# A tile's sums of exponentials taken one turn ahead on VectorE, in a linear-attention and token-mixing block

## The chip, the cores and the metric

The kernel runs on one core of a Trainium2 chip. Its time is the device time of one execution in microseconds. The engines are TensorE (PE in the profile, with its weight loads as PEld), VectorE (DVE), ScalarE (ACT), GpSimd (POOL) and SyncE (SP), which issues most of the transfers. Each engine works through its own instructions in order and waits on semaphores for the others.

## What is computed

The input is x, 2048 tokens of 512 channels. The block adds a linear attention and then a token-mixing MLP, each to its own input, each behind a layer norm:

```python
q, k, v = split_heads(layernorm(x) @ wqkv)          # 32 heads of 16
pq, pk = q @ w_phi, k @ w_phi                       # per head
phi_q = concat(softmax(pq), softmax(-pq))           # 32 features; phi_k likewise
kv = phi_k^T v;  z = phi_k^T 1
o = (phi_q kv) / (phi_q z + 1e-6)
h = x + o @ wo
h2 = h + transpose(gelu(transpose(layernorm(h)) @ w1 + b1) @ w2 + b2)
```

What matters here is phi_q. For each token and head there are two softmaxes over 16 numbers, one of pq and one of -pq. Each needs an extreme (the largest, or the smallest, logit), the exponentials of the shifted logits, and their sum.

## The kernel before, in words

Tokens are cut into 16 tiles of 128. Every large product is made of three fp32r matmuls (high by high, high by low, low by high; `mm3`, lines 64 to 68), so most operands exist as a high part, written by ScalarE as a copy, and a low part, the difference, which is subtracted on VectorE or GpSimd.

A first stage makes k and v for all tiles, and q for the first ones. A second, the attention stage, is the loop at lines 711 to 755, in which this change lies. Behind it come the rest of the first MLP product and the whole second one, which take more than half of the time and are not touched.

The loop goes over `it` from 0 to 17; one pass is called a turn here. Inside it the order of TensorE, VectorE, ScalarE and GpSimd is the order in which the program is written (`manual_schedule`, line 447); only SyncE's transfers are placed by the scheduler. A turn works on several tiles at once:

- TensorE: the numerators `pn` of tile it-1 (`s_num`, line 591), the transposes `tr` of tile it's features (`s_tr`, 575), then one piece of work: half of a q projection (`q_half`, 692), or a tile's part of the first MLP product (`fill`, 678). Then `po`, the output projection of tile it-1 (`s_wo`, 609), and the rest of the work. `pn` and `po` share one PSUM buffer, so `po` waits until `ol` has read `pn`, and the next turn's `pn` waits until `h` has read `po`.
- ScalarE: the moments of tile it-2's h, `oh` (the high part of `pn`, 602), `pht` (the copy of the transposes, 582), the exponentials of one q tile (`q_exp`, 247), the normalized `hn` and its high part `hs` (636), and the high parts `whi` of streamed weights (`his`, 648).
- GpSimd: the division of tile it+1's features by their denominators (`s_pq`, 496: `eq<-eq,w`), `r` (634), the product `ez` of tile it+3's features with z (471), the low part of `hs` (line 62), and the shift of the negative logits (`negate`, 169).
- VectorE: for turns 0 to 4, 6 and 8 a q tile's two extremes and the shift (`logit_ops`, 151; lines 165, 166, 159). In each turn `ol`, the low part of the numerators (607). `wlo`, the low part of streamed weights (659). The two sums of a tile's exponentials (`q_sum`, 225: the instructions `smq<-eq` of line 230). The denominators of tile it+2 (`s_den`, 475: six instructions, the first `tr<-ez` at 486, the last `w` at 494), which read the sums of that tile. Then `h`, the residual sum of tile it-1 (623).

`flush(left)` and `flush(1)` issue the `wlo` of weights whose high part was ordered before: the first those left from the turn before, the second one more at the end of the turn.

The order of VectorE is what the change touches. `q["sum"]` counts the tiles whose sums were issued; six are taken in the first stage and one ahead of the loop, so the loop takes tiles 7 to 15. Their exponentials are made well before: tile 7's ahead of the loop, tile 8's in turn 1, tile 15's in turn 10. In turns 5 to 13 the sums of tile it+2 are taken just ahead of the denominators that use them:

```python
sm = q_sums(0) if q["sum"] <= it + 2 else []
ol = s_ol(it - 1) if 0 <= it - 1 < NT else []
run(ql[:2] + ol + ql[2:] if ql else sm[:1] + ol)
flush(left)
run(sm if ql else sm[1:])
```

So a turn with extremes runs: extreme, extreme, `ol`, shift, left `wlo`, sum, sum, denominators, `h`, `wlo`. A turn without: sum, `ol`, left `wlo`, sum, denominators, `h`, `wlo`.

Of the kernel before, what the change touches and what calls it, by code (L numbers as in the profile page):

```python
# [37 lines left out]
def block_kernel(ctx: ExitStack, tc: tile.TileContext, x, xT, wT, phic, wo, w1, b1, w2, b2,  # L38
# [130 lines left out]
    def negate():  # L169

        if MN:
            ev, mx, mn = MN.pop(0)
            nc.gpsimd.tensor_sub(mn, mn, mx)
            nc.gpsimd.tensor_sub(ev[:, :, 1], mn.unsqueeze(3).to_broadcast([P, NPR, 2, DH]), ev[:, :, 0])

    def turns(*lists):

        return [ops[i] for i in range(max(map(len, lists))) for ops in lists if i < len(ops)]

    def run(*lists):  # L180
        for op in turns(*lists):
            op()
# [42 lines left out]
    def q_sum(t):  # L225

        assert t < SUMS or t - SUMS in W, "a tile's sums would go where others are still wanted"
        SQ[t] = sums[:, t % SUMS]
        e = signs(EQ[t])
        return [lambda c=c: nc.vector.reduce_sum(SQ[t][:, :, 1 - c], e[:, :, c], axis=AX.X) for c in range(2)]  # L230

    q = {"mm": 0, "logits": 0, "exp": 0, "sum": 0}
# [6 lines left out]
    def q_logits(lag):  # L239
        n = q["logits"]  # L240
        if n < min(NT, q["mm"] - lag + NT * (q["mm"] == NT)):
            EQ[n] = big.tile([P, NG, P], F32, name="eq", tag="big")
            q["logits"] += 1
            return logit_ops(PS[n], EQ[n], n >= Q_EARLY)
        return []

    def q_exp(lag):
        n = q["exp"]
        if n < min(NT, q["logits"] - len(MN) - lag):
            exps(n, EQ[n])  # L250
            q["exp"] += 1

    def q_sums(lag):
        n = q["sum"]
        if n < min(NT, q["exp"] - lag + NT * (q["exp"] == NT)):
            q["sum"] += 1
            return q_sum(n)
        return []
# [212 lines left out]
    def s_ez(t):  # L471
        EZ[t] = az.tile([P, NG, P], F32, name="ez")
        nc.gpsimd.tensor_mul(EZ[t], EQ[t], zB)  # L473
# [22 lines left out]
    def s_pq(t):  # L496
        nc.gpsimd.tensor_mul(heads(EQ[t]), heads(EQ[t]), W[t].rearrange("p g c h -> p (g c h)").unsqueeze(2).to_broadcast([P, 2 * H, DH]))  # L497
# [77 lines left out]
    def s_tr(t):  # L575
        PHT[t] = ak.tile([P, NG, P], F32, name="pht")
        ptr = ps_t.tile([P, 8, P], F32, name="tr").rearrange("p (r c) (a s) -> p r (c a) s", r=2, a=2)
        for g in range(NG):
            for r, rows in enumerate(HALF):
                nc.tensor.transpose(ptr[:, r, g, :], EQ[t][rows, g, :], ident[rows, rows])  # L580
        for r in range(2):
            nc.scalar.activation(PHT[t][:, :, r * 64:r * 64 + 64], ptr[:, r], AF.Copy)

    def s_kv():

        pt = banks("pt")[:, 0, 0:2]
        for b in range(2):
            nc.tensor.transpose(pt[:, b, :], kvS[:, 2 * b:2 * b + 2, :].rearrange("p n f -> p (n f)"), ident)
        nc.scalar.activation(kvB, pt, AF.Copy)

    def s_num(t):

        pn = banks("pn")[:, :, 0:2]
        for b in range(2):
            for c in range(4):
                for r, rows in enumerate(HALF):
                    cols = slice(32 * c, 32 * c + 32)
                    nc.tensor.matmul(pn[cols, r, b, :], kvB[rows, b, cols], PHT[t][rows, 4 * b + c, :],
                                     start=True, stop=True, skip_group_check=True)
        oh = ak.tile([P, 2, 2, P], F32R, name="oh")  # L600
        ol = ak.tile([P, 2, 2, P], F32R, name="ol")
        nc.scalar.activation(oh, pn, AF.Copy)
        OS[t] = oh, ol, pn

    def s_ol(t):
        oh, ol, pn = OS[t]
        return [lambda: nc.vector.tensor_sub(ol, pn, oh)]

    def s_wo(t):
        oh, ol, _ = OS.pop(t)  # L610
        PO[t] = po = banks("po")[:, 0].rearrange("p a s -> p (a s)")
        for j in range(4):
            mm3(po, oh[:, j // 2, j % 2, :], ol[:, j // 2, j % 2, :], woh[:, j, :], wol[:, j, :], j == 0, j == 3)

    def s_x(t):
        HT[t] = ak.tile([P, D], F32, name="h", bufs=4)
        nc.sync.dma_start(HT[t], x[t * P:(t + 1) * P, :])
# [8 lines left out]
    def s_moments(t):  # L626

        junk = ak.tile([P, D], F32, name="hj", bufs=1)
        nc.scalar.activation(VE[t][:, 1:2], VE[t][:, 2:3], AF.Copy, scale=-1.0 / D)
        nc.scalar.activation(junk, HT[t], AF.Square, bias=VE[t][:, 1:2], accum_out=VE[t][:, 3:4])  # L630
        nc.scalar.activation(VE[t][:, 0:1], VE[t][:, 3:4], AF.Identity, scale=(1.0 + EPS) / D, bias=eps2)

    def s_rstd(t):
        nc.gpsimd.tensor_tensor(r2[:, t:t + 1], VE[t][:, 0:1], mhalf[:, :1], op=ALU.pow)

    def s_hn(t):
        hn = ak.tile([P, D], F32, name="hn")
        nc.scalar.activation(VE[t][:, 1:2], VE[t][:, 1:2], AF.Copy, scale=r2[:, t:t + 1])
        nc.scalar.activation(hn, HT[t], AF.Identity, scale=r2[:, t:t + 1], bias=VE[t][:, 1:2])
        HN[t] = big.tile([P, 2, D], F32R, name="hs", tag="big")  # L640
        split(HN[t][:, 0], HN[t][:, 1], hn, nc.gpsimd)
# [6 lines left out]
    def his():  # L648
        while COMING:
            LATER.append(COMING.pop(0))  # L650
            _, raw, wh_ = LATER[-1]
            nc.scalar.activation(wh_, raw, AF.Copy)  # L652

    def flush(n=None):
        if n is None:
            his()
        for _ in range(len(LATER) if n is None else min(n, len(LATER))):
            wl_, raw, wh_ = LATER.pop(0)
            LO.append(nc.vector.tensor_sub(wl_, raw, wh_).ins)  # L659
# [18 lines left out]
    def fill(p, pool=None):  # L678

        t = FN[p]  # L680
        FN[p] = t + 1
        if FL[p] <= t:
            fill_load(p)
            flush()
        if t == 0:
            PU[p] = [pool.tile([P, D], F32, name="pu", tag="pu") for _ in range(2)]
        a, b = WI[p, t - t % 2]
        for c in range(2):
            DONE[0] = mm3(PU[p][c], a[:, t % 2, c * P:(c + 1) * P], b[:, t % 2, c * P:(c + 1) * P],
                HN[t][:, 0], HN[t][:, 1], t == 0, t == NT - 1)  # L690
# [9 lines left out]
    def turn(it):  # L700

        halves = Q_TURNS[it] if it < len(Q_TURNS) else ()
        n = [FN[0] <= it - LAG and FN[0] < NT, min(2, max(0, it - LAG + 1 - FN[1])) if q["logits"] == NT else 0]
        for p in range(2):
            ahead = n[p] + 1 + p + 2 * (it == NT)
            if it >= (LAG - 1, len(Q_TURNS) - 1)[p] and FL[p] < min(NT, FN[p] + ahead):
                fill_load(p)
        return ([lambda i=i: q_half(i) for i in halves] + [lambda: fill(0, ps_f)] * n[0]
                + [lambda: fill(1, ps_q)] * n[1])

    for it in range(NT + 2):
        if it < NT:
            s_x(it)
        shifted = q["logits"] - len(MN)
        ql = q_logits(0)
        work = turn(it)
        if it > NT:
            his()
        if 0 <= it - 2 < NT:
            s_moments(it - 2)  # L720
        if 0 <= it - 1 < NT:
            s_num(it - 1)
        if it < NT:
            s_tr(it)
        if it + 1 < NT:
            s_pq(it + 1)
        for w in work[:1]:
            w()
        if it == 0:
            s_kv()  # L730
        if q["exp"] < shifted:
            q_exp(0)
        if 0 <= it - 2 < NT:
            s_rstd(it - 2)
        if it + 3 < NT:
            s_ez(it + 3)
        if 0 <= it - 2 < NT:
            s_hn(it - 2)
        negate()
        left = len(LATER)  # L740
        his()
        sm = q_sums(0) if q["sum"] <= it + 2 else []
        ol = s_ol(it - 1) if 0 <= it - 1 < NT else []
        run(ql[:2] + ol + ql[2:] if ql else sm[:1] + ol)
        flush(left)
        run(sm if ql else sm[1:])
        if it > 0 and it + 2 < NT:
            run(s_den(it + 2, ps_t, "tr"))
        if 0 <= it - 1 < NT:
            s_wo(it - 1)  # L750
        for w in work[1:]:
            w()
        if 0 <= it - 1 < NT:
            s_h(it - 1)
        flush(1)
    flush()
    ms.close()
    a2.close()
# [305 lines left out]
```

## Time and profile before

| what | us |
|---|---|
| median of 3 runs | 520.4 (519.5 to 520.58) |
| the profiled execution | 519.79 |
| its span, first to last instruction | 518.0 |
| TensorE busy | 512.9 |
| VectorE busy | 394.0 |
| ScalarE busy | 285.4 |
| GpSimd busy | 235.2 |

The span is the time from the first instruction to the last; the profiled execution took 1.79 us more around it. Busy times overlap each other. The mean granted TensorE clock was 0.999 of full speed. The attention loop lies between about 138 and 262 us of the span. Rows of a time order begin with the start and the duration in microseconds, then engine, line, operation, and what is written from what; in brackets stands the idle time of that engine before it and what ended it. Turn n is taken to begin when TensorE loads the weights for `pn` in it.

### The profile page before, as it was taken

How to read it: one execution, taken by the hardware profiler on the slowest of the kernel's cores; microseconds unless marked ns; L12 is line 12 of the kernel's file. 1: busy time of each engine (PE TensorE's matmuls, PEld its weight loads, DVE VectorE, ACT ScalarE, POOL GpSimd, SP SyncE). 2: the span in 40 equal slices, each digit the busy share in tenths (PEclk: the TensorE clock that was granted, in tenths of full speed). 3: DMA queues.
4: the chain of work that ended last, by engine and by line, in shares of the span. 5: the costliest groups of instructions: out<-in, count | busy, mean ns of one | idle time of the engine just before them, and what ended most of it. 6: DMA issues, size and time to landing. Idle time of an engine off the chain costs nothing.

```text
span 518.0 us, 9761 instructions
## 1 busy us (share of the span) xinstructions
PE 512.9 (99%) x3761; PEld 433.8 (84%) x3761; DVE 394.0 (76%) x717; ACT 285.4 (55%) x500; POOL 235.2 (45%) x181
## 2 busy tenths in 40 slices
PE   9999999999999999999999999999999999999997
PEld 8888888888877777777788888888899999999997
DVE  6799889989987899697335624625797899888983
ACT  6999853526267877767756423425464434433530
POOL 2579997876999999974224000000001202110210
PEclk9999999999999999999999999999999999999999
DMA  8642301021403334333255433532134587567632
GB/s 306 213 142 84 102 22 42 1 81 42 126 27 97 103 103 119 107 103 124 82 163 162 122 94 90 183 101 63 40 116 98 136 202 139 141 151 180 135 50 61
DMA packets 46493, 57.66 MB, mean 111 GB/s; under 512 B 4080, under 2 KB 33136, under 8 KB 46448
## 3 DMA queue, kind: packets, MB, share of 16 engines
q1 hardware_dynamic: 43136, 51.38, 31.7%
q0 software_dynamic: 3024, 5.51, 8.1%
q8 instruction: 29, 0.48, 0.4%
q10 hardware_dynamic: 288, 0.17, 0.1%
q14 instruction: 16, 0.13, 0.1%
HBM read 46.81 MB, written 10.22 MB: 110 GB/s over the span
## 4 chain that ended last, share of the span: by engine, by line
PE 97%; DVE 1%; ACT 1%; issue 0%; DVEq 0%
PE pu L66 13%; PE pu L67 12%; PE pu L68 12%; PE py L910 11%; PE py L902 10%; PE py L913 6%; PE po L66 3%; PE pk_ps L66 3%; PE po L68 3%; PE po L67 3%; PE pk_ps L67 3%; PE pk_ps L68 3%; PE pv L67 3%; PE pv L68 3%; PE pv L66 3%; PE tr L580 2%
## 5 line engine op out<-in xcount | busy, mean ns | idle before, releaser
L980 POOL DMA_DIRECT2D out<-ot x14 | 12.4, 939 | 169.5 <-DVE ot L961 169.5
L66 PE MATMUL pu<-hs,whi 128*128 128x512 f32 x224 | 87.7, 394 | 0.0
L67 PE MATMUL pu<-hs,whi 128*128 128x512 f32 x224 | 87.2, 389 | 0.0
L68 PE MATMUL pu<-hs,wlo 128*128 128x512 f32 x224 | 86.5, 389 | 0.0
L659 DVE TENSOR_TENSOR wlo<-wraw,whi 128x512 fp32r<-128x512 f32 x56 | 46.6, 837 | 46.2 <-ACT whi L652 46.0
L864 ACT ACTIVATE whi<-wraw 128x1792 fp32r<-128x1792 f32 x26 | 44.0, 1704 | 31.2 <-issue 17.1
L652 ACT ACTIVATE whi<-wraw 128x512 fp32r<-128x512 f32 x56 | 34.6, 625 | 44.4 <-PE pu L67 39.4
L864 DVE TENSOR_TENSOR wlo<-wraw,whi 128x1792 fp32r<-128x1792 f32 x26 | 52.4, 2018 | 0.0
L66 PEld LDWEIGHTS pu<-hs,whi 128*128 128x128 f32 x224 | 42.0, 188 | 9.2 <-ACT hj L630 0.2
L68 PEld LDWEIGHTS pu<-hs,wlo 128*128 128x128 f32 x224 | 42.0, 188 | 8.8
L67 PEld LDWEIGHTS pu<-hs,whi 128*128 128x128 f32 x224 | 42.1, 188 | 8.5
L910 PE MATMUL py<-uf,whi 128*128 128x512 f32 x175 | 48.3, 395 | 0.0
L473 POOL TENSOR_TENSOR ez<-eq,zB 128x1024 f32<-128x1024 f32 x16 | 38.4, 2404 | 3.8 <-ACT zB L533 3.8
L902 PE MATMUL py<-uf,whi 128*128 128x256 f32 x210 | 39.0, 283 | 0.0
L209 POOL TENSOR_TENSOR pk<-pk,sk 128x1024 f32<-128x1024 f32 x16 | 31.0, 1937 | 11.2 <-DVE sk L208 6.5
L497 POOL TENSOR_TENSOR eq<-eq,w 128x1024 f32<-128x1024 f32 x16 | 32.4, 2024 | 3.2 <-DVE w L494 3.2
L910 PEld LDWEIGHTS py<-uf,whi 128*128 128x128 f32 x175 | 30.1, 189 | 3.9
L902 PEld LDWEIGHTS py<-uf,whi 128*128 128x128 f32 x210 | 32.8, 192 | 0.0
L213 POOL TENSOR_TENSOR zacc<-zacc,pk 128x1024 f32<-128x1024 f32 x13 | 31.2, 2402 | 0.5
L913 PEld LDWEIGHTS py<-uf,wlo 128*128 128x128 f32 x175 | 27.1, 189 | 3.8
L902 PE MATMUL py<-uf,wlo 128*128 128x256 f32 x105 | 29.7, 283 | 0.0
L913 PE MATMUL py<-uf,wlo 128*128 128x256 f32 x175 | 28.7, 281 | 0.0
(198 smaller groups left out, 1301.4 us busy)
## 6 DMA issues: line engine op xcount, KB each, us to landing
wraw<-in_w SPq DMA_DIRECT2D x112, 256.0 KB, 3.1
xraw<-in_xT SPq DMA_DIRECT2D x16, 256.0 KB, 2.8
xh<-in_x SPq DMA_DIRECT2D x16, 256.0 KB, 2.6
h<-in_x SPq DMA_DIRECT2D x16, 256.0 KB, 2.7
out<-h SPq DMA_DIRECT2D x16, 256.0 KB, 2.0
out<-ot POOLq DMA_DIRECT2D x14, 256.0 KB, 4.3
wraw<-in_wT SPq DMA_DIRECT2D x12, 256.0 KB, 4.9
out<-low POOLq DMA_DIRECT2D x7, 256.0 KB, 4.3
```

The costliest lines, as they stand in the source:

```text
L66: nc.tensor.matmul(o, ah, bh, start=first, stop=False)
L67: nc.tensor.matmul(o, ah, bl, start=False, stop=False)
L68: return nc.tensor.matmul(o, al, bh, start=False, stop=last).ins
L213: nc.gpsimd.tensor_add(zacc, zacc, PK[t])
L473: nc.gpsimd.tensor_mul(EZ[t], EQ[t], zB)
L497: nc.gpsimd.tensor_mul(heads(EQ[t]), heads(EQ[t]), W[t].rearrange("p g c h -> p (g c h)").unsqueeze(2).to_broadcast([P, 2 * H, DH]))
L652: nc.scalar.activation(wh_, raw, AF.Copy)
L659: LO.append(nc.vector.tensor_sub(wl_, raw, wh_).ins)
L864: in_order(lambda: nc.scalar.activation(wh_, raw, AF.Copy), lambda: nc.vector.tensor_sub(wl_, raw, wh_))
L902: in_order(lambda: nc.tensor.matmul(o, x[:, m[0]], UB[p, m[1]][:, y], start=opens and p == 0 and i == 0, stop=closes and p == NP - 1 and i ...
L910: in_order(lambda: nc.tensor.matmul(o, wh_[:, m[0]], UB[p, m[1]], start=p == 0, stop=False, skip_group_check=True))
L913: in_order(lambda: nc.tensor.matmul(o[:, 0], wl_[:, m[0]], UB[p, m[1]][:, 0], start=False, stop=p == NP - 1, skip_group_check=True))
```

## The change

The two sums of a tile are taken a turn earlier, and at the very end of VectorE's turn, behind `h` and the last `wlo`. Tile it+3 stands in the condition for it+2, so the sums are taken in turns 4 to 12. In a turn whose predecessor took sums, `ol` stands behind one extreme and not two, where there are extremes (turns 6 and 8); where there are none, `ol` is the first of the turn.

```diff
+    ahead = 2
     for it in range(NT + 2):
...
         his()
-        sm = q_sums(0) if q["sum"] <= it + 2 else []
+        sm = q_sums(0) if q["sum"] <= it + 3 else []
         ol = s_ol(it - 1) if 0 <= it - 1 < NT else []
-        run(ql[:2] + ol + ql[2:] if ql else sm[:1] + ol)
+        run(ql[:ahead] + ol + ql[ahead:])
+        ahead = 1 if sm else 2
         flush(left)
-        run(sm if ql else sm[1:])
         if it > 0 and it + 2 < NT:
             run(s_den(it + 2, ps_t, "tr"))
...
         flush(1)
+        run(sm)
     flush()
```

The order after it: extreme, `ol`, extreme, shift, left `wlo`, denominators, `h`, `wlo`, sum, sum in a turn with extremes; `ol`, left `wlo`, denominators, `h`, `wlo`, sum, sum in a turn without.

## The prediction

> **What bounds the kernel now.** First the page: what was busy, and the chain of work that ended last.
>
> ```profile
> span 518.0 us, 9761 instructions
> PE 512.9 (99%) x3761; PEld 433.8 (84%) x3761; DVE 394.0 (76%) x717; ACT 285.4 (55%) x500; POOL 235.2 (45%) x181
> ...
> PE 97%; DVE 1%; ACT 1%; issue 0%; DVEq 0%
> ```
>
> TensorE sets the end, and the change gives it neither more nor less to do. VectorE matters only where TensorE waits for it, so the second view is the time order of TensorE's weight loads. A turn of the attention loop begins with the load for `pn`. These are turns 6 to 10 and 12 to 14, with two loads for `po` between:
>
> ```profile
> 178.40 0.40 PEld L598 LDWEIGHTS pn<-pht,kvB 64*32 64x32 f32 x32 [0.35 <-ACT ve L629]
> 185.56 0.43 PEld L598 LDWEIGHTS pn<-pht,kvB 64*32 64x32 f32 x32 [0.61 <-ACT whi L652]
> 192.52 0.40 PEld L598 LDWEIGHTS pn<-pht,kvB 64*32 64x32 f32 x32 [0.35 <-ACT ve L629]
> 195.19 0.19 PEld L66 LDWEIGHTS po<-woh,oh 128*128 128x128 f32 x1 [0.20 <-DVE ol L607]
> 200.84 0.40 PEld L598 LDWEIGHTS pn<-pht,kvB 64*32 64x32 f32 x32 [0.35 <-issue]
> 203.34 0.19 PEld L66 LDWEIGHTS po<-woh,oh 128*128 128x128 f32 x1
> 209.12 0.40 PEld L598 LDWEIGHTS pn<-pht,kvB 64*32 64x32 f32 x32 [0.35 <-issue]
> 225.67 0.40 PEld L598 LDWEIGHTS pn<-pht,kvB 64*32 64x32 f32 x32 [0.35 <-ACT ve L629]
> 228.46 0.19 PEld L66 LDWEIGHTS po<-woh,oh 128*128 128x128 f32 x1 [0.33 <-DVE ol L607]
> 234.16 0.40 PEld L598 LDWEIGHTS pn<-pht,kvB 64*32 64x32 f32 x32 [0.35 <-issue]
> 241.09 0.40 PEld L598 LDWEIGHTS pn<-pht,kvB 64*32 64x32 f32 x32 [0.35 <-ACT ve L629]
> ```
>
> A gap of 0.35 before `pn` stands in nearly every turn, whoever is named, so it is no wait for VectorE. The lengths tell more. Turn 13 takes 6.93 us and turn 9 (six wide matmuls more) 8.28. Against these, turn 6 takes 7.16 (0.23 lost), turn 7 6.96 (0.03), turn 8 8.32 (0.04) and turn 12 8.49 (0.21). **About 0.5 us is all that VectorE costs TensorE in these turns**; that is the ceiling of any gain. In an unhindered turn `po` is loaded 2.50 after `pn` (203.34 - 200.84). In turn 12 it came 2.79 after, 0.29 late, for a loss of 0.21, so about 0.1 of a late `po` is absorbed.
>
> **What VectorE does there.** Third view: the time order of VectorE, turns 5 to 10, cut to what the sum uses (`mx`, `mn` are the extremes, `smq` the sums, `tr<-ez` opens the denominators, `h` ends them, `wlo` is the weights' low part).
>
> ```profile
> 177.15 0.69 DVE L623 SCALAR_TENSOR_TENSOR h<-po,h 128x512 f32<-128x512 f32 x1 [0.44 <-PE po L68]
> 177.77 0.08 DVE L623 DVE_READ_ACCUMULATOR h<-po,h 128x1 f32 x1
> 177.77 0.69 DVE L165 TENSOR_REDUCE mx<-pu 128x32 f32<-128x512 f32 x1
> ...
> 179.81 0.69 DVE L607 TENSOR_TENSOR ol<-pn,oh 128x512 fp32r<-128x512 f32 x1 [0.75 <-ACT oh L602]
> ...
> 181.01 1.27 DVE L230 TENSOR_REDUCE smq<-eq 128x32 f32<-128x512 f32 x2
> 182.20 1.22 DVE L486 TENSOR_REDUCE tr<-ez 128x64 f32<-128x1024 f32 x1
> ...
> 184.61 0.22 DVE L494 TENSOR_TENSOR w<-smq,tr 128x64 f32<-128x64 f32 x1
> 184.75 0.68 DVE L623 SCALAR_TENSOR_TENSOR h<-po,h 128x512 f32<-128x512 f32 x1
> ...
> 185.36 1.50 DVE L659 TENSOR_TENSOR wlo<-wraw,whi 128x512 fp32r<-128x512 f32 x1
> 186.78 0.67 DVE L230 TENSOR_REDUCE smq<-eq 128x32 f32<-128x512 f32 x1
> 187.38 0.69 DVE L607 TENSOR_TENSOR ol<-pn,oh 128x512 fp32r<-128x512 f32 x1
> 187.98 0.68 DVE L230 TENSOR_REDUCE smq<-eq 128x32 f32<-128x512 f32 x1
> ...
> 191.88 1.45 DVE L659 TENSOR_TENSOR wlo<-wraw,whi 128x512 fp32r<-128x512 f32 x1
> 193.26 0.68 DVE L165 TENSOR_REDUCE mx<-pu 128x32 f32<-128x512 f32 x1
> ...
> 194.46 0.67 DVE L607 TENSOR_TENSOR ol<-pn,oh 128x512 fp32r<-128x512 f32 x1
> ...
> 202.24 0.69 DVE L607 TENSOR_TENSOR ol<-pn,oh 128x512 fp32r<-128x512 f32 x1 [0.49 <-ACT oh L602]
> 202.85 0.68 DVE L659 TENSOR_TENSOR wlo<-wraw,whi 128x512 fp32r<-128x512 f32 x1
> ...
> 210.53 0.69 DVE L607 TENSOR_TENSOR ol<-pn,oh 128x512 fp32r<-128x512 f32 x1 [1.81 <-ACT oh L602]
> ```
>
> A 512-wide operation takes 0.60 from start to start. The `wlo` at 185.36 and 191.88 take 1.50 and 1.45, the one at 202.85 only 0.68. GpSimd and ScalarE in time order say why:
>
> ```profile
> 185.03 1.28 POOL L62 TENSOR_TENSOR hs<-hn,hs 128x512 fp32r<-128x512 f32 x1
> ...
> 191.50 1.29 POOL L62 TENSOR_TENSOR hs<-hn,hs 128x512 fp32r<-128x512 f32 x1
> ...
> 202.91 1.03 POOL L634 TENSOR_TENSOR r<-ve,mhalf 128x1 f32<-128x1 f32 x1
> 203.91 2.41 POOL L473 TENSOR_TENSOR ez<-eq,zB 128x1024 f32<-128x1024 f32 x1
> ...
> 209.33 1.94 POOL L497 TENSOR_TENSOR eq<-eq,w 128x1024 f32<-128x1024 f32 x1
> 211.23 0.55 POOL L634 TENSOR_TENSOR r<-ve,mhalf 128x1 f32<-128x1 f32 x1
> 211.74 2.40 POOL L473 TENSOR_TENSOR ez<-eq,zB 128x1024 f32<-128x1024 f32 x1
> ```
>
> ```profile
> 184.45 0.62 ACT L652 ACTIVATE whi<-wraw 128x512 fp32r<-128x512 f32 x1
> ```
>
> **`wlo`, with both inputs in SBUF, and a GpSimd operation run one after the other.** The `hs` at 185.03 ends at 186.31 and `wlo` 0.55 later (186.86); the `hs` at 191.50 ends at 192.79 and `wlo` 0.54 later. At 202.85 `wlo` was first, and `r` took 1.03 in place of the 0.55 at 211.23. After a wait VectorE's next operation starts 0.47 behind GpSimd's end (186.78 - 186.31).
>
> **The change part by part.** It adds and removes no operation. Two sums (1.19, from 181.01 to 182.20) leave turns 5 to 13 and stand at the end of turns 4 to 12, past everything after `ol`, and behind the last `wlo`. Their inputs were exponentiated at least a turn earlier, so no wait is added. No DMA moves; SP and GpSimd keep their order. Where tile 14 or 15 has its extremes (turns 6 and 8), the second extreme goes behind `ol`, 0.60. Between the end of one turn and `ol` there stood one sum, or two extremes; now there stand two sums, or two sums and one extreme: **0.60 more in front of `ol`, free where VectorE idles there for `oh`, paid where it does not.** Behind `ol`, `h` comes 0.60 earlier. What is queued behind a late `ol` is TensorE's `po`, at once.
>
> *Turn 5* idles for `oh` as turn 6 does, so the first moved sums cost nothing there; without that idle time they would cost 0.60. *Turn 6*, a gain: the sums of tile 8 run from 177.76 to 178.95, one extreme to 179.55, and `ol` still waits for `oh` until 179.81. Behind it two sums are gone and one extreme is added, so `h` is at 184.75 - 0.59 = 184.16. Turn 7 can start at 178.40 + 6.93 = 185.33, not 185.56: **-0.23**.
>
> *Turn 7*, a loss: the `wlo` behind that `h` waits for `whi`, ready at 184.45 + 0.62 = 185.07, and GpSimd's `hs` has started at 185.03. So it still ends at 186.86. Two sums from 186.78, then `ol` at 187.98 (where the second sum stood) instead of 187.38, ending at 188.67, `po` 0.06 behind (turn 8: 194.46 + 0.67 to 195.19), so 188.73. TensorE would have been ready at 185.33 + 2.50 = 187.83. **0.90 late, 0.8 lost**. Together +0.57 at the start of turn 8: 193.1.
>
> *Turn 8*: `h` of turn 7 is 0.6 later and `wlo` asks at 192.5, still inside the `hs` that ends at 192.79. So the next operation starts at 193.26 as before; two sums and one extreme give `ol` at 195.05, not 194.46. This 0.59 is the delay that TensorE already has; it is not paid twice. Turn 9 starts at 200.84 + 0.59 = **201.43**.
>
> *Turn 9* decides. `oh` sets `ol` there, 1.40 after `pn` (202.24 - 200.84), so 202.83, and `wlo` follows at 203.44, not 202.85. GpSimd's `r` at 202.91 now runs free, and `ez` follows 0.51 later (211.74 - 211.23), at 203.42. **`ez` is ahead by 0.02**, and my own estimate of turn 9's start is no better than 0.05 (see A). If `ez` goes first, VectorE is blocked until 203.42 + 2.40 = 205.82 and goes on at 206.29. Denominators take 2.55 (182.20 to 184.75): `h` at 208.84, `w` done at 206.29 + 2.41 + 0.22 = 208.92, and `eq<-eq,w` with its 1.94 starts about 0.15 later, up to 211.01. The `wlo` behind `h` asks at 209.45, inside it, and VectorE goes on at 211.48. Two sums, then `ol` at 212.67, ending at 213.36, `po` at 213.42. TensorE, in turn 10 from 201.43 + 8.28 = 209.71, wanted it at 212.21: 1.21 late, **1.1 lost**, +1.7 in all. After that `oh` sets `ol` again, and turn 12 with its input 1.7 later does not pay its 0.21: **+1.5 at turn 13**, and TensorE carries it to the end.
>
> The Trainium skill ("SBUF — State Buffer", Who interferes with whom) says that a VectorE instruction with two SBUF inputs excludes a GpSimd one that reads SBUF, and that the order of issue decides which of them waits for the whole of the other. By that rule turn 9 costs its full 1.1 however small the lead, and the sum is +1.5; if the two shared the port evenly, `wlo` would lose at most its own 0.68, which turn 9 can absorb, and the sum would stay near +0.6. The trace agrees with the rule in both orders: 1.50 for `wlo` at 185.36, 1.03 for `r` at 202.91.
>
> **The sum.** The profiled execution took 519.79, a span of 518.0 and 1.79 around it. -0.2 + 0.8 + 1.1 - 0.2 = +1.5 gives a span of 519.5, a time of 521.3. The runs' median is 520.4, 0.6 above that execution and inside their spread of 1.1; on the median the forecast is **521.9**.
>
> **Rivals.** *A, 0.33:* `wlo` goes ahead of `ez` in turn 9. Then `r` or `ez` gives way by half a microsecond as before, and turns 10 to 12 run as now, 0.6 later: +0.6, **521.0**. For it: the margin is as small as my error in turn 9's start. Against it: in turn 12 the next turn began 5.70 behind a late `po` (234.16 - 228.46), and 5.70 behind turn 8's at 195.05 + 0.67 + 0.06 = 195.78 would be 201.48, which makes turn 9 later if anything. *B, the other side, 0.10:* `wlo` of turn 6 starts before `hs`. It decides at 185.03 against 185.07. Then the sums end at 186.9, before `ol` is due at 187.38 or TensorE at 187.83, turn 7 pays nothing, and if the like happens at 191.50 all the stalls go: -0.5, **519.9**. Against it: GpSimd is busy without a pause up to 185.03, and `whi` hangs on none of the moved work. *C, 0.12:* a second full collision in turns 11 to 13, or an order of transfers behind the loop that suits TensorE less: +2.2 to +3, **523**. *D:* that the sums do not move or wait for their exponentials: excluded by the program's order. The forecast has 0.45.
>
> The range 520.1 to 522.8 takes in A, the forecast, and half of B and C with the runs' own scatter of 0.4. 0.2% is 1.04 us, about what a measurement of this kernel can tell from no change; B's full gain is below it, A's loss too. Slower: 0.45 x 0.85 + 0.33 x 0.15 + 0.12 x 0.8 = 0.53. Faster: a third of B and scatter of A, 0.06. Same: 0.41.
>
> **What would show it.** In the changed profile: turn 7 starts about 0.23 earlier (185.3); `wlo` of turn 6 still ends near 186.86, followed by two sums and then `ol`; `po` in turn 7 names `ol` with a wait near 0.9; turn 9's `wlo` of about 3 us, and `po` of turn 10 over 1 us late; turns 13 and on at their present lengths. I am wrong if `wlo` of turn 6 ends before 186, if `po` in turn 7 does not wait, or if time changes ahead of turn 5 or behind turn 14.

## The result, and the profile after

| | before | changed |
|---|---|---|
| median of 13 runs each, us | 519.92 (519.5 to 520.58) | 521.29 (520.18 to 521.98) |
| profiled execution, us | 519.79 | 521.14 |
| its span | 518.0 | 519.4 |

The changed kernel is slower: the ratio to before is 1.0021, with a 95% interval of 1.0014 to 1.0028, that is 0.7 to 1.5 us. (The two medians alone give 1.0026. The ratio stands nearer to that of the means, 521.17 and 520.00, since the runs of the changed kernel are not one group.) Three of its 13 runs lie between 520.18 and 520.32, ten between 521.02 and 521.98. The experiments bear on what divides them.

The first view is again the time order of TensorE's weight loads, in the changed kernel: the `pn` that begin turns 6 to 14, and the `po` that waited for `ol`.

```profile
178.20 0.40 PEld L598 LDWEIGHTS pn<-pht,kvB 64*32 64x32 f32 x32 [0.35 <-ACT ve L629]
185.10 0.40 PEld L598 LDWEIGHTS pn<-pht,kvB 64*32 64x32 f32 x32 [0.35 <-ACT ve L629]
188.53 0.19 PEld L66 LDWEIGHTS po<-woh,oh 128*128 128x128 f32 x1 [0.96 <-DVE ol L607]
192.83 0.40 PEld L598 LDWEIGHTS pn<-pht,kvB 64*32 64x32 f32 x32 [0.35 <-ACT ve L629]
195.61 0.19 PEld L66 LDWEIGHTS po<-woh,oh 128*128 128x128 f32 x1 [0.32 <-DVE ol L607]
201.32 0.40 PEld L598 LDWEIGHTS pn<-pht,kvB 64*32 64x32 f32 x32 [0.35 <-ACT hj L630]
209.61 0.40 PEld L598 LDWEIGHTS pn<-pht,kvB 64*32 64x32 f32 x32 [0.35 <-issue]
213.21 0.19 PEld L66 LDWEIGHTS po<-woh,oh 128*128 128x128 f32 x1 [1.14 <-DVE ol L607]
218.92 0.40 PEld L598 LDWEIGHTS pn<-pht,kvB 64*32 64x32 f32 x32 [0.35 <-issue]
227.21 0.40 PEld L598 LDWEIGHTS pn<-pht,kvB 64*32 64x32 f32 x32 [0.35 <-issue]
235.47 0.40 PEld L598 LDWEIGHTS pn<-pht,kvB 64*32 64x32 f32 x32 [0.35 <-issue]
242.39 0.40 PEld L598 LDWEIGHTS pn<-pht,kvB 64*32 64x32 f32 x32 [0.35 <-ACT ve L629]
```

Differences of these rows are the turns' lengths. Turn 6 now takes 6.90 us (7.16 before), turn 7 7.73 (6.96), turn 8 8.49 (8.32), turn 9 8.29 (8.28), turn 10 9.31 (8.26), turn 11 8.29 (8.29), turn 12 8.26 (8.49), turn 13 6.92 (6.93). Together that is -0.26 + 0.77 + 0.17 + 0.01 + 1.05 - 0.23 - 0.01 = +1.50. TensorE waits for `ol` for about 1 us in turn 7 and in turn 10, where it did not wait before.

VectorE in time order, changed kernel, turns 6 to 10:

```profile
183.96 0.68 DVE L623 SCALAR_TENSOR_TENSOR h<-po,h 128x512 f32<-128x512 f32 x1
...
184.93 1.76 DVE L659 TENSOR_TENSOR wlo<-wraw,whi 128x512 fp32r<-128x512 f32 x1 [0.28 <-ACT whi L652]
186.62 1.27 DVE L230 TENSOR_REDUCE smq<-eq 128x32 f32<-128x512 f32 x2
187.81 0.67 DVE L607 TENSOR_TENSOR ol<-pn,oh 128x512 fp32r<-128x512 f32 x1
...
192.20 0.98 DVE L659 TENSOR_TENSOR wlo<-wraw,whi 128x512 fp32r<-128x512 f32 x1
193.10 1.26 DVE L230 TENSOR_REDUCE smq<-eq 128x32 f32<-128x512 f32 x2
194.29 0.68 DVE L165 TENSOR_REDUCE mx<-pu 128x32 f32<-128x512 f32 x1
194.89 0.67 DVE L607 TENSOR_TENSOR ol<-pn,oh 128x512 fp32r<-128x512 f32 x1
...
202.73 0.69 DVE L607 TENSOR_TENSOR ol<-pn,oh 128x512 fp32r<-128x512 f32 x1 [0.51 <-ACT oh L602]
203.33 2.92 DVE L659 TENSOR_TENSOR wlo<-wraw,whi 128x512 fp32r<-128x512 f32 x1
...
208.73 0.68 DVE L623 SCALAR_TENSOR_TENSOR h<-po,h 128x512 f32<-128x512 f32 x1
...
209.33 2.04 DVE L659 TENSOR_TENSOR wlo<-wraw,whi 128x512 fp32r<-128x512 f32 x1
211.29 1.27 DVE L230 TENSOR_REDUCE smq<-eq 128x32 f32<-128x512 f32 x2
212.48 0.68 DVE L607 TENSOR_TENSOR ol<-pn,oh 128x512 fp32r<-128x512 f32 x1
```

And GpSimd beside it:

```profile
184.87 1.27 POOL L62 TENSOR_TENSOR hs<-hn,hs 128x512 fp32r<-128x512 f32 x1
186.11 2.39 POOL L497 TENSOR_TENSOR eq<-eq,w 128x1024 f32<-128x1024 f32 x1
...
202.79 0.54 POOL L634 TENSOR_TENSOR r<-ve,mhalf 128x1 f32<-128x1 f32 x1
203.31 2.40 POOL L473 TENSOR_TENSOR ez<-eq,zB 128x1024 f32<-128x1024 f32 x1
...
208.89 1.94 POOL L497 TENSOR_TENSOR eq<-eq,w 128x1024 f32<-128x1024 f32 x1
```

`h` of turn 6 comes 0.8 us earlier than before by the span, 0.6 by the turn. But `wlo` behind it waits for `whi`, finds `hs` at work since 184.87 and ends at 184.93 + 1.76 = 186.69, 8.49 behind the start of turn 6 and so at the same place as before (8.46). The two sums follow, and `ol` only then, at 187.81. In turn 9 `ez` starts at 203.31 and `wlo` at 203.33: 0.02 us behind, and it takes 2.92 in place of 0.68. The next `wlo`, at 209.33, starts inside `eq<-eq,w`, and `ol` of turn 10 stands behind it and the two sums, 1.95 later than before.

### The profile page after: what moved, and what is told of

Read it like the earlier page. It is cut to its first block, busy times and chain, and to the rows that moved or that the text cites. A ratio compares the mean times of both kernels' runs of the same rounds, so it can differ in the third digit from the quotient of the medians.

```text
span 519.4 us, 9761 instructions
## 1 busy us (share of the span) xinstructions
PE 512.9 (99%) x3761; PEld 433.0 (83%) x3761; DVE 397.4 (77%) x717; ACT 285.4 (55%) x500; POOL 234.3 (45%) x181
## 4 chain that ended last, share of the span: by engine, by line
PE 92%; ACT 2%; POOL 2%; DVE 2%; DMA 1%; issue 0%; SPq 0%; DVEq 0%
PE pu L66 12%; PE pu L67 12%; PE pu L68 12%; PE py L912 11%; PE py L904 10%; PE py L915 6%; PE pk_ps L66 3%; PE pk_ps L67 3%; PE pv L66 3%; PE pk_ps L68 3%; PE pv L67 3%; PE pv L68 3%; PE po L66 2%; PE po L67 2%; PE po L68 2%; PE kvp L221 1%
## 5 line engine op out<-in xcount | busy, mean ns | idle before, releaser
L659 DVE TENSOR_TENSOR wlo<-wraw,whi 128x512 fp32r<-128x512 f32 x56 | 49.4, 886 | 46.7 <-ACT whi L652 46.5
L904 PE MATMUL py<-uf,wlo 128*128 128x256 f32 x105 | 29.7, 283 | 0.0
L62 POOL TENSOR_TENSOR hs<-hn,hs 128x512 fp32r<-128x512 f32 x16 | 21.2, 1323 | 17.6 <-ACT hs L61 17.6
```

Source lines behind the costliest of these rows:

```text
L904: in_order(lambda: nc.tensor.matmul(o, x[:, m[0]], UB[p, m[1]][:, y], start=opens and p == 0 and i == 0, stop=closes and p == NP - 1 and i ...
```

## The experiments

Theory: the loss has two parts, both made by `wlo`, which took turns with GpSimd wherever the two met in the rows above. The sums stand behind it and ahead of `ol` (turns 7 and 8), and a delay of half a microsecond lets `wlo` meet `ez` (turn 9, paid in turn 10). Rivals: `ol` behind two sums costs a little in every turn and that is all; or VectorE's work as such delays TensorE.

The starts of turn 1 differ by up to 1.1 us between the profiles (142.18 to 143.27), and the runs of before spread by as much, so that spread comes from the stages ahead of the loop. From the start of turn 1 to the end of the profiled execution it is 377.30 us before and 378.86 in the changed kernel: behind the loop nothing of the loss is won back. For that reason the table has, beside the medians, the time from the `pn` of turn 4 to that of turn 15 in the profile, which leaves it out. Before: 164.58 to 247.99, 83.41 us.

Each ratio is to the runs of before that were taken beside that kernel.

| kernel | median, us | ratio to before, 95% interval | turn 4 to 15, us | against before |
|---|---|---|---|---|
| changed | 521.29 | 1.0021 (1.0014 to 1.0028) | 84.92 | +1.51 |
| changed, small GpSimd operation | 520.64 | 1.0012 (1.0004 to 1.0021) | 84.02 | +0.61 |
| changed, sums ahead of wlo | 519.28 | 0.9984 (0.9976 to 0.9993) | 82.83 | -0.58 |
| changed, ol behind both extremes | 521.55 | 1.0029 (1.0016 to 1.0041) | 84.90 | +1.49 |
| changed, sums ahead of wlo in turn 6 | 521.9 | 1.0037 (1.0025 to 1.005) | 84.86 | +1.45 |
| the same in turns 6 and 7 | 519.7 | 0.9996 (0.9987 to 1.0005) | 83.27 | -0.14 |
| before without the sums | 520.06 | 0.9999 (0.999 to 1.0008) | 83.25 | -0.16 |
| before, one sum more ahead of wlo | 520.67 | 1.0013 (1.0003 to 1.0023) | 84.94 | +1.53 |
| before, one sum more behind wlo | 520.0 | 0.9998 (0.9989 to 1.0006) | 83.47 | +0.06 |

**A small operation that holds `ez` back.**

```diff
+            if it == 9:
+                nc.gpsimd.tensor_sub(mhalf[:, 1:2], mhalf[:, 2:3], mhalf[:, 3:4])
             s_ez(it + 3)
```

> The changed kernel with one 128x1 subtraction more on GpSimd in turn 9, between r and ez; it reads and writes spare columns. Theory (two costs: ol behind both sums in turn 7, and in turn 9 ez taking GpSimd's turn 0.02 us ahead of wlo): the small operation holds ez back by 0.2 to 0.4 us, wlo of turn 9 goes first and takes under 1 us in place of 2.92, turn 10 falls from 9.31 to about 8.3, and the kernel with more work is 0.9 us faster than the changed one: +0.5 to +0.6 us against before. Rival (all of the loss is ol queued behind the two sums, paid in several turns): the small operation changes nothing, +1.4 us against before.

VectorE and GpSimd in turn 9, in time order:

```profile
204.29 0.72 DVE L659 TENSOR_TENSOR wlo<-wraw,whi 128x512 fp32r<-128x512 f32 x1
```

```profile
204.27 0.19 POOL L738 TENSOR_TENSOR mhalf<-mhalf 128x1 f32<-128x1 f32 x1
204.43 2.86 POOL L473 TENSOR_TENSOR ez<-eq,zB 128x1024 f32<-128x1024 f32 x1
```

`wlo` waits for 0.19 us of GpSimd work and not for 2.40, and goes ahead of `ez`, which takes 2.86. Turn 10 falls from 9.31 to 8.26; turn 12 pays again (8.44 for 8.26). The kernel with 0.19 us more to do is 0.90 us shorter over these turns and 0.65 in the median. So turn 10's loss is this meeting, and 0.61 is the price of the other part.

**The sums ahead of the last `wlo`.**

```diff
-        flush(1)
         run(sm)
+        flush(1)
```

> The changed kernel with the two sums ahead of the turn's last wlo and not behind it. Theory: the sums have one SBUF input and run beside GpSimd, so they fill the time that wlo waits for GpSimd's hs; wlo of turn 6 still ends at about 186.7, but ol follows it at once, at 186.8 and not 187.8. Turn 7 back at 6.9 (7.73 in the changed kernel), turn 9's left wlo asks before r and does not meet ez, turns 6 and 12 without their losses: -0.3 to -0.5 us against before, 1.7 to 1.9 us below the changed kernel. Rival (taking the sums a turn ahead costs by itself, wherever they stand at the turn's end): +1 us or more against before, as the changed kernel.

VectorE, then GpSimd, at the end of turn 6 and in turn 7:

```profile
185.37 1.27 DVE L230 TENSOR_REDUCE smq<-eq 128x32 f32<-128x512 f32 x2
186.56 0.95 DVE L659 TENSOR_TENSOR wlo<-wraw,whi 128x512 fp32r<-128x512 f32 x1
187.50 0.69 DVE L607 TENSOR_TENSOR ol<-pn,oh 128x512 fp32r<-128x512 f32 x1
```

```profile
185.68 1.28 POOL L62 TENSOR_TENSOR hs<-hn,hs 128x512 fp32r<-128x512 f32 x1
```

This kernel's loop runs 0.8 later in its span than that of the changed one. The sums run while `hs` does, at their usual length. `wlo` then waits a quarter of a microsecond, not one, and ends at 187.51, 0.55 behind `hs` as ever; `ol` follows at once. Every turn from 6 to 13 takes its shortest time, within 0.01 (6.90, 6.93, 8.26, 8.29, 8.25, 8.29, 8.26, 6.93). It is the one version whose interval lies clear below before: 0.9984, or -0.4 to -1.2 us, which takes in the -0.58 of the turns. So taking the sums a turn ahead is not what costs; their place behind `wlo` is.

**One sum more in the kernel before, on either side of `wlo`.** In turn 9 the first sum is taken twice; the second time changes no value.

```diff
         run(ql[:2] + ol + ql[2:] if ql else sm[:1] + ol)
+        if it == 9:
+            run(sm[:1])
         flush(left)
```

> The kernel before, with one sum of turn 9 taken twice: the repeated 0.60 us stands between ol and the left wlo. Theory: wlo asks at 203.45 in place of 202.85, ez starts at 203.42, so wlo takes about 2.9 us; h of turn 9 comes at 209.4, later than TensorE's 209.1, the next wlo meets eq<-eq,w, ol of turn 10 comes near 212.7 (210.53 before): +1.3 to +1.7 us for 0.60 us of VectorE work. If wlo still goes first, 0. Rival (VectorE has slack in turn 9, 0.49 idle there and h 2.5 us ahead of its use): 0 to +0.1.

```diff
         flush(left)
+        if it == 9:
+            run(sm[:1])
```

> The same repeated sum as in the run with the sum before wlo, but just behind the left wlo of turn 9. Theory: wlo asks at 202.85 as before and goes ahead of r and ez; the 0.60 us is absorbed (h of turn 9 at 207.2, used at 209.1): 0 to +0.1 us against before. Rival (0.60 us of VectorE work delays the chain of turn 9 to 10 wherever it stands): as much as with the sum ahead of wlo.

Behind `wlo` the 0.60 us costs nothing (0.9998; +0.06 over the turns). Ahead of it the 12 runs fall into six of 519.79 to 520.39 and six of 520.95 to 522.09, and the median between them says little. I had expected one outcome or the other, not both. The same kernel was profiled twice more:

> The kernel with the repeated sum before wlo once more, unchanged, for its profile. Its 12 runs fell into six of 519.8 to 520.4 and six of 521.0 to 522.1, and the one profile is of the second kind (wlo of turn 9 2.93 us). Theory (the two groups are the two outcomes of one meeting): a profile of a run near 520 has wlo of turn 9 under 1 us, r or ez longer by what it waits, and turns 9 and 10 of 8.3; a profile of a run above 521 has wlo of 2.9 us. Rival (the groups come from the rest of the kernel): a run near 520 shows wlo of 2.9 us too.

> As the first repetition: the length of wlo of turn 9, 0.7 or 2.9 us, goes with the group of the run's time.

The first took 521.68 us, the second 519.67. `wlo` of turn 9, and `ez`, in the first:

```profile
203.93 2.91 DVE L659 TENSOR_TENSOR wlo<-wraw,whi 128x512 fp32r<-128x512 f32 x1
```

```profile
203.89 2.40 POOL L473 TENSOR_TENSOR ez<-eq,zB 128x1024 f32<-128x1024 f32 x1
```

and in the second:

```profile
203.29 0.68 DVE L659 TENSOR_TENSOR wlo<-wraw,whi 128x512 fp32r<-128x512 f32 x1
```

```profile
203.30 2.94 POOL L473 TENSOR_TENSOR ez<-eq,zB 128x1024 f32<-128x1024 f32 x1
```

One program, two outcomes: `ez` 0.04 us ahead, and `wlo` waits for all of it; `wlo` 0.01 ahead, and `ez` waits 0.5. With the first profile of this kernel (522.09 us, `wlo` 2.93), the length of `wlo` goes with the group in all three, so the two groups of runs are the two outcomes of this meeting.

**The changed kernel, twice more**, for the three runs near 520.3.

> The changed kernel once more, for its profile. Three of its 13 runs were at 520.2 to 520.3, ten at 521.0 to 522.0. Theory: the three are the runs in which wlo went ahead of ez in turn 9; a run near 520.3 has wlo of turn 9 under 1 us and turn 10 of 8.3, a run above 521 has 2.9 us and 9.3. Rival: both groups show 2.9 us.

> As the first repetition of the changed kernel: about one run in four with wlo of turn 9 under 1 us.

Both fell into the upper group (521.94 and 521.16), with a `wlo` of 2.94 and 2.90 and a turn 10 of 9.3. No profile of a run near 520.3 was had. That `wlo` won in those three is inferred, from the kernel above and from the small operation, whose 520.27 to 521.23 has no group near 522. Since that kernel, with `wlo` first, reaches 521.23 itself, one or two of the ten upper runs may be of its kind too. In the three profiles of the changed kernel the time from the start of turn 1 is 378.86, 378.72 and 378.71 us, so a run of 520.3 with `ez` first would need turn 1 at 141.6, earlier than in any profile.

**`ol` behind both extremes again.**

```diff
-        ahead = 1 if sm else 2
```

> The changed kernel with ol behind both extremes again (turns 6 and 8); the sums stay at the end of the turn before. It undoes the second part of the change alone. Theory (the loss is set at fixed points of GpSimd's timetable): ol of turn 8 is 0.60 later and turn 8 some 0.6 longer (9.1), but wlo of turn 9 meets ez in any case and VectorE goes on when ez has ended, so turn 10 pays 0.5 less (8.7 or 8.8 for 9.31): +1.4 us against before, as the changed kernel. Rival (delays of ol add up): 0.6 more than the changed kernel, +2.0.

Turn 8 takes 9.05 (8.49), turn 10 8.72 (9.31), the sum of the turns is that of the changed kernel. VectorE and GpSimd in turn 9:

```profile
204.35 2.35 DVE L659 TENSOR_TENSOR wlo<-wraw,whi 128x512 fp32r<-128x512 f32 x1
```

```profile
203.73 2.42 POOL L473 TENSOR_TENSOR ez<-eq,zB 128x1024 f32<-128x1024 f32 x1
```

`wlo` is 0.62 behind `ez`, and no longer a near thing: none of the six runs is under 521.16. The second part of the change, `ol` behind one extreme, saves 0.56 in turn 8, and turn 10 takes it back.

**The sums ahead of `wlo` in some turns only.**

```diff
-        flush(1)
-        run(sm)
+        if it == 6:
+            run(sm)
+        flush(1)
+        if it != 6:
+            run(sm)
```

> The changed kernel with the sums ahead of the last wlo in turn 6 alone. It takes away the cost that was seen in turn 7. Theory: turn 7 takes 6.9, but wlo of turn 7 still ends with GpSimd's hs, two sums and an extreme behind it, so ol of turn 8 comes at the same time, turn 8 takes 9.2 for 8.49, turn 9's start and its meeting with ez are as they were: +1.4 us against before, nothing gained. Rival (turn 7 and turn 10 are two separate costs): 0.8 less than the changed kernel, +0.6.

and with `it in (6, 7)`:

> The changed kernel with the sums ahead of the last wlo in turns 6 and 7 alone. Theory: turns 7 and 8 take their shortest times, turn 9 starts before 200.9, its left wlo asks before r and goes ahead, turn 10 takes 8.3. Turn 12 pays instead: wlo of turn 11 ends with GpSimd's eq<-eq,w at a time that does not depend on the half microsecond won, with two sums ahead of ol: turn 12 near 8.7. Against before -0.2 to +0.1 us. Rival (the gain of the kernel with all sums first comes from turns 6 and 7): -0.5 to -0.8, as that kernel.

In turn 6 alone: turn 7 takes 6.93 (7.73) and turn 8 9.26 (8.49); turns 7 and 8 together 16.19, against 16.22. VectorE in turns 7 and 8:

```profile
192.25 1.77 DVE L659 TENSOR_TENSOR wlo<-wraw,whi 128x512 fp32r<-128x512 f32 x1
193.95 1.27 DVE L230 TENSOR_REDUCE smq<-eq 128x32 f32<-128x512 f32 x2
...
195.73 0.67 DVE L607 TENSOR_TENSOR ol<-pn,oh 128x512 fp32r<-128x512 f32 x1
```

```profile
192.19 1.29 POOL L62 TENSOR_TENSOR hs<-hn,hs 128x512 fp32r<-128x512 f32 x1
```

`wlo` comes earlier in its turn, 0.06 us behind `hs`, and waits the longer: the 0.8 us won is lost a turn later. In the median this kernel is 0.6 above the changed one, in its turns it is not; it has no runs in the lower group, and only five runs. With turns 6 and 7 both, the meeting in turn 9 goes, and turn 12 pays as expected (8.65), because `wlo` of turn 11 waits for `eq<-eq,w`. VectorE, then GpSimd:

```profile
224.09 2.10 DVE L659 TENSOR_TENSOR wlo<-wraw,whi 128x512 fp32r<-128x512 f32 x1
226.12 1.26 DVE L230 TENSOR_REDUCE smq<-eq 128x32 f32<-128x512 f32 x2
227.31 0.67 DVE L607 TENSOR_TENSOR ol<-pn,oh 128x512 fp32r<-128x512 f32 x1
```

```profile
223.71 1.94 POOL L497 TENSOR_TENSOR eq<-eq,w 128x1024 f32<-128x1024 f32 x1 [1.44 <-DVE w L494]
```

**The kernel before without the loop's sums.**

```diff
-        sm = q_sums(0) if q["sum"] <= it + 2 else []
+        if q["sum"] <= it + 2 and q_sums(0):
+            SQ[q["sum"] - 1] = SQ[q["sum"] % 6]
+        sm = []
```

> The kernel before without the loop's sums: turns 5 to 13 leave out the two sums, 10.7 us of VectorE work in all, and the denominators of tiles 7 to 15 use other tiles' sums. Theory: turn 6's loss of 0.23 goes, but wlo of turn 7 still ends when GpSimd's hs allows, with two extremes and ol behind it, so turn 8 gives it back (8.6 or 8.7 for 8.32); only turn 12's 0.2 is gained: -0.1 to -0.3 us, less than the kernel with all the sums ahead of wlo. Rival (VectorE's work as such costs TensorE): every loss goes, -0.5 or more, below the kernel with the sums ahead of wlo.

Without 10.7 us of VectorE work the time is that of before: 0.9999, with an interval that holds the theory's -0.1 to -0.3 us and ends at -0.5, where the rival began. The median alone does not tell the two apart; the turns do, with -0.16. Turns 6 and 12 gain 0.26 and 0.23, and turn 8 takes 8.68 (8.32): VectorE and GpSimd there:

```profile
192.35 1.75 DVE L659 TENSOR_TENSOR wlo<-wraw,whi 128x512 fp32r<-128x512 f32 x1
...
195.22 0.67 DVE L607 TENSOR_TENSOR ol<-pn,oh 128x512 fp32r<-128x512 f32 x1
```

```profile
192.27 1.29 POOL L62 TENSOR_TENSOR hs<-hn,hs 128x512 fp32r<-128x512 f32 x1
```

The kernel with all its sums, placed ahead of `wlo`, is 0.42 us faster over these turns than the one with none (82.83 against 83.25). In these turns VectorE's amount of work is not what TensorE waits for; its order against GpSimd is.

## Why the prediction was right

- *The ceiling* of about 0.5 us: the version with every turn at its shortest gains 0.58 in these turns.
- *Turn 6*, -0.23 forecast: -0.26 measured.
- *Turn 7*, 0.8 lost: 0.77, by the mechanism given. Where the sums stand ahead of `wlo`, turn 7 has no loss.
- *Turn 8*, "not paid twice": 0.17 of it was paid. From the start of turn 6 to that of turn 9 the kernel lost 0.68 (23.12 against 22.44), where the prediction had 0.59; rival A's reckoning with 5.70 behind a late `po` had pointed to 0.05 more. That reckoning was the better one: turn 9 began 5.71 behind turn 8's `po` (201.32 - 195.61), and that `po`, counted from the start of turn 6, was itself 0.03 later than worked out. This was the step that was mis-sized.
- *Turn 9*: `ez` ahead of `wlo` by 0.02 forecast, by 0.02 measured in the profile. That figure was luck as much as working: turn 9's start was 0.09 later than worked out, and GpSimd's `ez` later by about the same. In the two further profiles the lead was 0.01 and 0.07. What was sound was that it is a near thing, with a chance for each side; most of the 13 runs went one way, three at least look like the other.
- *Turn 10*, 1.1 lost: 1.05. *Turn 12*, -0.2: -0.23. *The sum*, +1.5: +1.50 by the turns and +1.4 by the span.
- *The time*, 521.9: 521.29 measured. 0.5 of the difference is the base: the median of three runs of before, 520.4, was above that of 13, 519.92; the forecast's other figure, 521.3 from the profiled execution's own time, was the better one, and its exact hit is luck: it started 0.13 below the median of before and left out the lower group of runs. That group is the rest of the difference, as the median of the ten upper runs, 521.40, is 1.48 above 519.92.
- *Rivals B and C* did not come: in turn 6 `hs` was ahead of `wlo` by 0.06 (0.04 forecast), and no second loss stands in turns 11 to 13.
- *By how much slower*: 0.7 to 1.5 us by the interval, so the bound of 0.2% lies inside it.

A thing that the prediction did not have: with the sums gone from behind `ol`, VectorE's denominators reach their PSUM bank before ScalarE has copied the transposes out of it. In the changed kernel's turn 5:

```profile
173.80 1.23 DVE L486 TENSOR_REDUCE tr<-ez 128x64 f32<-128x1024 f32 x1 [0.43 <-ACT pht L582]
...
176.95 0.69 DVE L623 SCALAR_TENSOR_TENSOR h<-po,h 128x512 f32<-128x512 f32 x1 [0.51 <-PE po L68]
```

Of the 0.60 that the denominators were to come earlier, 0.43 was spent waiting there. It cost nothing, since `h` of that turn waits for TensorE anyway, 0.51 here.

## What to carry to other kernels

Before moving work on VectorE, mark the operations that take turns with GpSimd (in this loop `wlo`, the only one on VectorE with both inputs in SBUF) and the GpSimd operations that they meet. A `wlo` that waits ends at a time that GpSimd sets. Work moved ahead of it was free here where it filled that wait (the sums first, at the end of turn 6). Work moved behind it cost 0.77 us where what TensorE needs stood next (turn 7), and nothing where VectorE had time to spare (the repeated sum in turn 9). The sums took their usual 1.27 us beside `hs`, so reductions like them are what to put ahead of the operation that has to wait. Where two operations that take turns become ready within some hundredths of a microsecond, forecast both outcomes, as one program can show both.

## What the runs showed of the hardware that was not expected

- The order in which `wlo` and a GpSimd operation run is settled by hundredths of a microsecond, and differs between executions of one program: 0.04 us of lead for `ez` gave a `wlo` of 2.91 us and a time of 521.68, 0.01 for `wlo` gave 0.68 and 519.67. The Trainium skill ("SBUF — State Buffer", Who interferes with whom) says that the order of issue decides who blocks; the runs agree, and add that with such margins one program gives both orders.
- 0.19 us of extra GpSimd work took 0.65 us off the median, and 0.60 us of extra VectorE work cost nothing on one side of `wlo` and about 1.5 us, in half of the 12 runs, on the other.
- A blocked instruction is busy in the profile: `wlo` is shown with 2.92 us of busy time, where it takes 0.68 when it goes first.
- A waiting `wlo` goes ahead of GpSimd's next operation: behind `hs`, which ends at 186.14, `eq<-eq,w` starts at 186.11 and takes 2.39 in place of the 1.94 at 208.89, while `wlo` ends 0.55 behind `hs`. So `wlo` waits for the one operation that it met, and not for all that GpSimd has queued; this is why 0.19 us of work could stand in for 2.40.
